# Choosing the passes of a fused attention and FFN kernel two ahead instead of one, with their scales made at the choice

## Chip, cores and metric

The kernel runs on one core of a Trainium2 chip. The metric is the device time of one execution in microseconds (us), as the median of several runs.

## What is computed

```python
# attention: 8 batches, 8 heads, 512 local + 32 global queries, head size 64
s_g  = scale * q_g @ concat(k_g, k_l).T          # global queries see all keys
s_l  = concat(scale * q_l @ k_g.T,               # local queries see the global keys
              where(|i - j| <= 32, scale * q_l @ k_l.T, -1e9))   # and a band of 65
out  = concat(sm(s_g) @ v_all, sm(s_l) @ v_gl)
# FFN on the 4352 rows x of 512 that come out of it
h = x @ w_in                                     # 512 -> 2048
g = where(h > 0, h, exp(min(h, 0)) - 1)          # ELU
return g @ w_out                                 # 2048 -> 512
```

## The kernel before

Attention and FFN run interleaved on the same engines. TensorE works in 16-bit floats for the FFN: every operand is split into a high and a low f16 part, and three products (high by high, high by low, low by high) are summed. That needs power-of-two scales: one for each block of x, one for each pair of f-tiles of the weights.

**The FFN's stream.** The rows of x make 17 blocks of 256: 16 of local rows and one (number 16) of all global rows. The 2048 columns of the middle layer are 8 steps of 256. A *pass* is one block through the steps of one *group*: "a" is step 0, "b" step 1, "c" steps 2 and 3, "d" steps 4 to 7, "f" all 8. While the weights are still being converted, the first blocks go through passes a, b, c, d, and each waits until the weights of its group are there (`group in tab`). Once the table of "f" exists, every block that has not begun takes one pass f. In a step `ffn1` fills a PSUM tile `h` with 24 matmuls (L300), ScalarE turns it into `g` and `hs` (L310, L311, both scaled by a column of the pass's scale tile `xs`), takes the exponential (L312), VectorE joins the two (L319), ScalarE makes the f16 high part `gh` (L326; in pass f L340 and L341) and VectorE the low part `gl` (L322). `ffn2`, two steps later, multiplies by the second weights (L376; L418 in pass f), and at the end of a pass the sum is scaled and stored (L384, L387).

**The scale tile.** `scales(group, mx)` makes the tile `xs` of a pass with four small GpSimd instructions of 128 partitions by 1 to 8 columns: L521 is what L310 waits for, L522 what L311 waits for, L524 what L326 (and L322) need, L525 what the end of the pass needs. They read the scale of the block (`xm`) and of the weights (`isc` of L217, `wm` and `t` of the group's table). Before, `xs` has four buffers, so a pass's tile has to wait until the pass four earlier has read its own for the last time.

**What sets the order.** `choose()` walks the blocks in order and gives the first one whose split is done and whose next group has a table; it calls `scales` at once. Before, it is called when the last step of the running pass has been issued, so one pass is known ahead. A scheduler then places each instruction in its engine's queue; `scales` is under a raised priority (AHEAD_OF), and each engine runs its queue strictly in that order. GpSimd's queue also holds L703 (it normalises the probabilities `p`, four of 128x224 a time, and TensorE transposes them in L714), L646 and L647 (the same for the global queries), L661 (a memset) and L162 (a clamp of 128x1024 in the conversion of the weights, which VectorE goes on with in L166, L169, L173 and ScalarE in L191).

Of the kernel before, what the change touches and what calls it, by code (L numbers as in the profile page):

```python
# [10 lines left out]
F32 = mybir.dt.float32  # L11
# [11 lines left out]
P = 128  # L23
# [6 lines left out]
NP = NFT // 2  # L30
# [26 lines left out]
def attn_ffn(ctx: ExitStack, tc: tile.TileContext, qT, qgT, kT, vT, w_in, w_out, mask, out):  # L57
# [5 lines left out]
    ffn = ctx.enter_context(tc.tile_pool(name="ffn", bufs=2))  # L63
# [220 lines left out]
    def ffn_stream():  # L284
# [228 lines left out]
            return xh, xl, mx, done  # L513

        def scales(group, mx):
            sc = ffn.tile([P, 3 * NP + 1], F32, name="xs", bufs=4)
            wm, t = tab[group]
            o = GROUPS[group]
            r = slice(*o)
            with tc.high_priority(offset=AHEAD_OF):  # L520
                nc.gpsimd.tensor_scalar(sc[:, r], isc[:, r], mx[:, 2:3], 1.0, ALU.mult, ALU.mult)  # L521
                nc.gpsimd.tensor_scalar(sc[:, 2 * NP + 1 + o[0]:2 * NP + 1 + o[1]], isc[:, r], mx[:, 2:3], -1.0,  # L522
                                        ALU.mult, ALU.mult)
                nc.gpsimd.tensor_scalar(sc[:, NP + o[0]:NP + o[1]], t[:, r], mx[:, 3:4], 1.0, ALU.mult, ALU.mult)  # L524
                nc.gpsimd.tensor_scalar(sc[:, 2 * NP:2 * NP + 1], wm, mx[:, 2:3], 2.0 ** -17, ALU.mult, ALU.mult)  # L525
            return sc

        order = [*range(NBL - 1), NBL, NBL - 1]
        xs = {}
        step = dict.fromkeys(order, 0)  # L530

        def load():
            if "f" in tab:
                n = state.setdefault("sums", 0)
                state["turn"] = not state.get("turn")
                if n < NP and state["turn"]:
                    add_up(n, False)
                    state["sums"] += 1
                n = state.setdefault("cross", 0)
                first = min((GROUPS["abcd"[step[b]]][0] for b in order if 0 < step[b] < 4), default=NP)  # L540
                if n < state["sums"] and not uses[n] and n < first:
                    add_up(n, True)
                    state["cross"] += 1
            for blk in order:
                if blk in ready and blk not in xs and not step[blk] and len(xs) < NX:
                    xs[blk] = split_x(blk)

        def choose():

            for blk in order:  # L550
                if blk in xs and xs[blk][3] and step[blk] < 4:
                    group = "f" if "f" in tab and not step[blk] else "abcd"[step[blk]]
                    if group in tab:
                        step[blk] += 4 if group == "f" else 1
                        xh, xl, mx, _ = xs[blk]
                        seven = [] if group == "f" else None
                        if seven is None:
                            for p in range(*GROUPS[group]):
                                uses[p] += 1
                        return group, blk, xh, xl, scales(group, mx), seven  # L560

        job = None
        left = 0
        while lead[0]:
            load()
            yield True
        while left <= NBL:
            load()
            job = job or choose()
            if job is None:  # L570
                yield True
                continue
            cur, job = job, None
            group, blk = cur[:2]
            lo, hi = GROUPS[group]
            for p in range(lo, hi):
                load()
                yield from ffn1(cur, p)
                if len(pend) > LAG2:
                    yield from ffn2()  # L580
                if p == hi - 1:
                    job = choose()
            if group in "df":
                del xs[blk]
                left += 1
# [226 lines left out]


    f = ffn_stream()
    units = (u for g in "abcd" for u in load_weights(g))
    done = credit = 0
# [93 lines left out]
```

## Time and profile before

| | |
|---|---|
| time, median of 3 runs | 995.57 us (993.61 to 997.8) |
| the profiled execution | 993.12 us, span 991.4 us |
| mean granted clock of TensorE | 0.991 |
| busy share of the span: TensorE / VectorE / ScalarE / GpSimd | 96% / 79% / 68% / 25% |

The time is that of a whole execution; the span goes from its first to its last instruction. The engines are named PE (TensorE matmuls), PEld (its weight loads), DVE (VectorE), ACT (ScalarE), POOL (GpSimd) and SP (the queue that issues most DMAs) in the rows below. "Idle before, <- X" in a row is the time for which the engine did nothing ahead of that instruction, and X is what ended it. A busy share is an average over stages with different limits.

### The profile page before, as it was taken

What the parts mean: (1) busy time and instruction counts of PE and PEld (TensorE: products, weight loads), DVE (VectorE), ACT (ScalarE), POOL (GpSimd) and SP (SyncE); (2) the same over time, 40 slices, a digit from 0 to 9 for tenths busy, and PEclk for the clock granted to TensorE, in tenths of its full rate; (3) what the DMA queues carried; (4) which work ended last, traced back from release to release, by engine and by line L of the source; (5) the groups of instructions that cost most, each with busy time, mean ns of one, the idle gap of its engine ahead of it and who ended that gap; (6) DMA issues with size and microseconds to landing.
All of it is one profiled execution on the core that took longest, in us unless ns stands there. A gap on an engine that the chain in (4) does not pass through costs nothing.

```text
span 991.4 us, 21656 instructions
## 1 busy us (share of the span) xinstructions
PE 954.0 (96%) x8128; PEld 767.2 (77%) x8128; DVE 786.9 (79%) x2233; ACT 678.0 (68%) x1545; POOL 251.8 (25%) x444
## 2 busy tenths in 40 slices
PE   7899879999999999999999999999999999999997
PEld 4576556666667888888888788888888888888886
DVE  5898989999987778787777778787787878776665
ACT  4978777886656666666756666667766766677664
POOL 2656444462311221212211122112211221100000
PEclk9799999999999999999999999999999999999999
DMA  8627665651211023011211023112210100000000
GB/s 282 234 81 264 201 192 185 224 175 44 92 59 59 34 80 107 28 44 70 81 49 28 33 81 108 28 39 75 81 44 13 43 23 33 1 23 22 2 23 22
DMA packets 39360, 81.95 MB, mean 83 GB/s; under 512 B 3896, under 2 KB 6328, under 8 KB 39256
## 3 DMA queue, kind: packets, MB, share of 16 engines
q1 hardware_dynamic: 39064, 80.31, 24.5%
q8 instruction: 64, 1.05, 0.4%
q14 instruction: 40, 0.33, 0.1%
q10 hardware_dynamic: 144, 0.13, 0.0%
q0 software_dynamic: 48, 0.13, 0.0%
HBM read 65.36 MB, written 15.20 MB: 81 GB/s over the span
## 4 chain that ended last, share of the span: by engine, by line
PE 64%; DVE 16%; ACT 10%; issue 6%; DMA 3%; POOL 1%; SPq 0%; POOLq 0%; DVEq 0%; ACTq 0%
PE h L300 24%; PE acc L418 10%; PE h L418 5%; PE pa L736 4%; PE acc L376 4%; PE pa L714 4%; PE pa L677 4%; ACT p L696 3%; PE pa L418 2%; DVE p L689 2%; PE pa L300 2%; PE pa L625 2%; DVE gl L322 2%; DVE g L319 2%; ACT g L310 1%
## 5 line engine op out<-in xcount | busy, mean ns | idle before, releaser
L300 PE MATMUL h<-xh,winh 128*128 128x256 f16 x992 | 271.5, 274 | 10.3 <-ACT hs L311 8.1
L300 PE MATMUL h<-xl,winh 128*128 128x256 f16 x992 | 271.0, 273 | 0.0
L300 PE MATMUL h<-xh,winl 128*128 128x256 f16 x992 | 270.9, 273 | 0.1
L300 PEld LDWEIGHTS <-winh 128*128 128x128 f16 x2176 | 211.4, 99 | 49.4 <-issue 18.1
L703 POOL TENSOR_SCALAR p<-p,sm 128x224 f32<-128x224 f32 x256 | 147.0, 592 | 321.5 <-DVE sm L701 142.2
L319 DVE SCALAR_TENSOR_TENSOR g<-g,hs 128x512 f32<-128x512 f32 x136 | 95.4, 702 | 91.1 <-ACT g L312 90.5
L696 ACT ACTIVATE p<-p,m 128x224 f32<-128x224 f32 x256 | 120.3, 473 | 65.9 <-DVE m L692 65.9
L418 PEld LDWEIGHTS <-gh 128*128 128x128 f16 x1456 | 141.8, 98 | 21.5 <-issue 4.8
L300 PEld LDWEIGHTS <-winl 128*128 128x128 f16 x1088 | 106.7, 98 | 13.5 <-DVE winl L194 0.5
L310 ACT ACTIVATE g<-h,xs 128x512 f32<-128x512 f32 x124 | 84.8, 683 | 45.7 <-PE h L300 40.4
L322 DVE SCALAR_TENSOR_TENSOR gl<-gs,xs,gh 128x640 f16<-128x640 f32 x104 | 94.3, 907 | 22.7 <-ACT gh L341 22.5
L341 ACT ACTIVATE gh<-gs,xs 128x640 f16<-128x640 f32 x104 | 86.3, 830 | 36.5 <-DVE gs L337 36.3
L340 ACT ACTIVATE gh<-g,xs 128x256 f16<-128x256 f32 x104 | 53.2, 512 | 84.4 <-DVE g L319 84.4
L418 PE MATMUL acc<-wouth,gh 128*128 128x256 f16 (+1 forms) x312 | 87.8, 282 | 0.2 <-ACT gh L341 0.2
L312 ACT ACTIVATE g<-g 128x512 f32<-128x512 f32 x136 | 85.7, 632 | 0.0
L311 ACT ACTIVATE hs<-h,xs 128x512 f32<-128x512 f32 x124 | 84.6, 682 | 1.1 <-POOL xs L522 1.1
L418 PE MATMUL acc<-wouth,gl 128*128 128x256 f16 x312 | 85.0, 273 | 0.2 <-DVE gl L322 0.2
L418 PE MATMUL acc<-woutl,gh 128*128 128x256 f16 x312 | 85.0, 273 | 0.0
L714 PE MATMUL pa<-ident,p 128*128 128x128 f32 x512 | 77.9, 277 | 4.4 <-POOL p L703 3.3
L418 PEld LDWEIGHTS <-gl 128*128 128x128 f16 x728 | 71.2, 98 | 12.9 <-DVE gl L322 0.5
L689 DVE CUSTOM_DVE_ANT_0 p<-pa,msk 128x224 f32<-128x224 f32 x228 | 76.9, 384 | 3.0 <-PE pa L677 3.0
L322 DVE SCALAR_TENSOR_TENSOR gl<-g,xs,gh 128x256 f16<-128x256 f32 (+1 forms) x136 | 76.5, 563 | 3.1 <-ACT gh L326 2.9
(206 smaller groups left out, 1952.4 us busy)
## 6 DMA issues: line engine op xcount, KB each, us to landing
v<-vT SPq DMA_DIRECT2D x64, 256.0 KB, 2.7
k<-kT SPq DMA_DIRECT2D x32, 448.0 KB, 4.3
q<-qT SPq DMA_DIRECT2D x32, 256.0 KB, 5.4
raw<-w_in SPq DMA_DIRECT2D x8, 1024.0 KB, 6.2
raw<-w_out SPq DMA_DIRECT2D x8, 1024.0 KB, 5.4
out<-o SPq DMA_DIRECT2D x32, 256.0 KB, 2.1
od<-o SPq DMA_DIRECT2D x24, 256.0 KB, 3.0
o<-od SPq DMA_DIRECT2D x24, 256.0 KB, 3.0
```

Source lines behind the costliest of these rows:

```text
L300: nc.tensor.matmul(h[:, j, :], wt[:, c, f], xt[:, c, :], start=k == 0, stop=k == 11)
L310: nc.scalar.activation(g, hf, AF.Relu, scale=sc[:, p:p + 1])
L311: nc.scalar.activation(hs, hf, AF.Copy, scale=sc[:, 2 * NP + 1 + p:2 * NP + 2 + p])
L312: nc.scalar.activation(g, g, AF.Exp, scale=-1.0)
L319: nc.vector.scalar_tensor_tensor(out=g, in0=g, scalar=-1.0, in1=hs, op0=ALU.add, op1=ALU.max)
L322: nc.vector.scalar_tensor_tensor(out=dst, in0=src, scalar=sg, in1=hi, op0=ALU.mult, op1=ALU.subtract)
L341: nc.scalar.activation(gh[:, 2:7, :], s, AF.Copy, scale=sg)
L418: nc.tensor.matmul(cols, gt, w, start=first, stop=last and k == len(todo) - 1)
L689: nc.vector.tensor_tensor_reduce(out=p[:, 0:KW], in0=sp[r][:, j * KW:(j + 1) * KW], in1=msk[:, mi, :], op0=ALU.add, op1=ALU.max, scale=1.0 ...
L696: nc.scalar.activation(ps[i][:, 0:KW], ps[i][:, 0:KW], AF.Exp, bias=m[:, 1, i:i + 1], scale=scale, accum_out=s[:, 0, i:i + 1])
L703: nc.gpsimd.tensor_scalar(ps[i][:, 0:KW], ps[i][:, 0:KW], s[:, 1, i:i + 1], 1.0, ALU.mult, ALU.mult)
L714: nc.tensor.transpose(tp[:, (2 * r + i) * P:(2 * r + i + 1) * P], ps[2 * j + r][:, i * P:(i + 1) * P], ident)
```

## The change

`scales` gets six buffers instead of four. The single `job` becomes a list `jobs` of up to two, which `look()` fills by calling `choose()` until there are two or none can be chosen. `look()` is called at the top of each round, right after a pass is taken from the list, and after the last step of a pass. So the scales of a pass are issued up to one whole pass earlier.

```diff
         def scales(group, mx):
-            sc = ffn.tile([P, 3 * NP + 1], F32, name="xs", bufs=4)
+            sc = ffn.tile([P, 3 * NP + 1], F32, name="xs", bufs=6)
...
-        job = None
+        jobs = []
         left = 0
+
+        def look():
+            while len(jobs) < 2:
+                job = choose()
+                if job is None:
+                    return
+                jobs.append(job)
+
...
         while left <= NBL:
             load()
-            job = job or choose()
-            if job is None:
+            look()
+            if not jobs:
                 yield True
                 continue
-            cur, job = job, None
+            cur = jobs.pop(0)
+            look()
             group, blk = cur[:2]
...
                 if p == hi - 1:
-                    job = choose()
+                    look()
```

In the order of the built programs TensorE's and VectorE's queues stay the same, instruction for instruction, and so does that of SP's DMAs. GpSimd's queue has the same instructions, moved in the first third of the program only; ScalarE's has one instruction moved. The three places below are all in the stage in which the weights are converted. In the names, `xm_308` is block 0, `xm_583` block 1, `xm_846` block 2; from L562 on the changed file's line numbers are up to 9 higher.

GpSimd, pass b of block 2 (`xs_1554`), before; it stands between two clamps of the weights:

```order
L162 TENSOR_SCALAR cu_1434<-cu_1434 128x1024
L521 TENSOR_SCALAR xs_1554<-isc_133,xm_846 128x1
L522 TENSOR_SCALAR xs_1554<-isc_133,xm_846 128x1
L524 TENSOR_SCALAR xs_1554<-t_b_1234,xm_846 128x1
L525 TENSOR_SCALAR xs_1554<-wm_b_1233,xm_846 128x1
L162 TENSOR_SCALAR cu_1550<-cu_1550 128x1024
```

The same pass's scales now (`xs_1419`), beside those of pass a of block 2 (`xs_1414`):

```order
L521 TENSOR_SCALAR xs_1414<-isc_133,xm_846 128x1
L521 TENSOR_SCALAR xs_1419<-isc_133,xm_846 128x1
L522 TENSOR_SCALAR xs_1414<-isc_133,xm_846 128x1
L522 TENSOR_SCALAR xs_1419<-isc_133,xm_846 128x1
L525 TENSOR_SCALAR xs_1414<-wm_a_392,xm_846 128x1
L524 TENSOR_SCALAR xs_1414<-t_a_393,xm_846 128x1
```

Its L521 and L522 moved some 15 instructions up, ahead of a group of L703; nothing stands between the two clamps any more.

ScalarE at the same pass, before (`h_1559` is block 2's step of pass b):

```order
L387 ACTIVATE o_1463<-acc_1461,xs_1028 128x512
L312 ACTIVATE g_1516<-g_1516 128x512
L310 ACTIVATE g_1593<-h_1559,xs_1554 128x512
L311 ACTIVATE hs_1594<-h_1559,xs_1554 128x512
L161 ACTIVATE cu_1550<-raw_1548 128x1024
L326 ACTIVATE gh_1521<-g_1516,xs_1485 128x512
```

And now:

```order
L387 ACTIVATE o_1473<-acc_1471,xs_973 128x512
L310 ACTIVATE g_1593<-h_1559,xs_1419 128x512
L311 ACTIVATE hs_1594<-h_1559,xs_1419 128x512
L312 ACTIVATE g_1521<-g_1521 128x512
L161 ACTIVATE cu_1555<-raw_1553 128x1024
L326 ACTIVATE gh_1526<-g_1521,xs_1414 128x512
```

The exponential L312 of the step before went behind L310 and L311 of this one.

GpSimd, the first pass c (block 0, `xs_1748`), before:

```order
L162 TENSOR_SCALAR cu_1794<-cu_1794 128x1024
L525 TENSOR_SCALAR xs_1748<-wm_c_1667,xm_308 128x1
L521 TENSOR_SCALAR xs_1748<-isc_133,xm_308 128x2
L522 TENSOR_SCALAR xs_1748<-isc_133,xm_308 128x2
L521 TENSOR_SCALAR xs_1908<-isc_133,xm_583 128x2
L522 TENSOR_SCALAR xs_1908<-isc_133,xm_583 128x2
```

And now, with the scales of passes c of blocks 1 and 2 (`xs_1753`, `xs_1758`) in the same place:

```order
L162 TENSOR_SCALAR cu_1804<-cu_1804 128x1024
L525 TENSOR_SCALAR xs_1748<-wm_c_1667,xm_308 128x1
L521 TENSOR_SCALAR xs_1748<-isc_133,xm_308 128x2
L521 TENSOR_SCALAR xs_1753<-isc_133,xm_583 128x2
L521 TENSOR_SCALAR xs_1758<-isc_133,xm_846 128x2
L522 TENSOR_SCALAR xs_1753<-isc_133,xm_583 128x2
L522 TENSOR_SCALAR xs_1758<-isc_133,xm_846 128x2
L522 TENSOR_SCALAR xs_1748<-isc_133,xm_308 128x2
```

L521 of block 0 keeps its place behind the clamp; its L522 moved from third to seventh in the row.

## Rows read from the trace of the kernel before

**Rows 1.** The page, busy time of the engines.
```profile
PE 954.0 (96%) x8128; PEld 767.2 (77%) x8128; DVE 786.9 (79%) x2233; ACT 678.0 (68%) x1545; POOL 251.8 (25%) x444
```
**Rows 2.** Stretches: us, busy us (instructions) of each engine, TensorE's granted clock, DMA.
```profile
core 0: us, PE busy (x) PEld busy (x) DVE busy (x) ACT busy (x) POOL busy (x), PEclk, DMA share, GB/s
120.00:130.00 10.00, 8.03 (x55) 4.87 (x54) 10.00 (x23) 6.17 (x10) 2.18 (x2) 1.00 0.78 242
...
170.00:200.00 30.00, 26.91 (x189) 17.83 (x187) 29.96 (x62) 25.41 (x49) 12.88 (x10) 1.00 0.62 204
...
250.00:300.00 50.00, 50.00 (x381) 35.08 (x380) 45.76 (x110) 30.04 (x77) 11.17 (x19) 1.00 0.24 79
```
**Rows 3.** ScalarE's waits for scales: us in total, times, longest us.
```profile
ACT g L310 <- POOL xs L521: 5.0, 2, 3.5
...
ACT hs L311 <- POOL xs L522: 1.1, 1, 1.1
```
**Rows 4.** Timeline of ScalarE at block 2's pass b: start us, us, instruction.
```profile
113.18 0.64 ACT L312 ACTIVATE g<-g 128x512 f32<-128x512 f32 x1
115.33 0.69 ACT L310 ACTIVATE g<-h,xs 128x512 f32<-128x512 f32 x1 [1.52 <-POOL xs L521]
...
118.72 0.70 ACT L326 ACTIVATE gh<-g,xs 128x512 f16<-128x512 f32 x1
```
**Rows 5.** Timeline of GpSimd, the same place.
```profile
113.46 1.84 POOL L521 TENSOR_SCALAR xs<-isc,xm 128x1 f32<-128x1 f32 x1 [4.47 <-ACT o L387]
```
**Rows 6.** Timeline of VectorE, the same place.
```profile
115.17 0.68 DVE L319 SCALAR_TENSOR_TENSOR g<-g,hs 128x512 f32<-128x512 f32 x1
...
119.45 1.02 DVE L322 SCALAR_TENSOR_TENSOR gl<-g,xs,gh 128x512 f16<-128x512 f32 x1 [0.68 <-ACT gh L326]
```
**Rows 7.** Timeline of SP, the load that L161 at 117.66 reads.
```profile
107.72 0.38 SPq L152 DMA_DIRECT2D raw<-w_out  x1
```
**Rows 8.** Tile raw, its loads from 90 to 150 us.
```profile
DMA to landing us min/median/max: 4.9/5.4/6.9
```
**Rows 9.** Timeline of GpSimd at the first pass c.
```profile
137.33 1.96 POOL L162 TENSOR_SCALAR cu<-cu 128x1024 f32<-128x1024 f32 x1
139.37 0.27 POOL L525 TENSOR_SCALAR xs<-wm_c,xm 128x1 f32<-128x1 f32 x1
139.60 0.27 POOL L521 TENSOR_SCALAR xs<-isc,xm 128x2 f32<-128x2 f32 x1
139.85 0.27 POOL L522 TENSOR_SCALAR xs<-isc,xm 128x2 f32<-128x2 f32 x1
```
**Rows 10.** Timeline of ScalarE, the same place.
```profile
139.91 0.69 ACT L310 ACTIVATE g<-h,xs 128x512 f32<-128x512 f32 x1 [3.50 <-POOL xs L521]
140.49 0.68 ACT L311 ACTIVATE hs<-h,xs 128x512 f32<-128x512 f32 x1
```
**Rows 11.** Timeline of TensorE, the same place.
```profile
141.22 0.37 PE L300 MATMUL h<-xh,winh 128*128 128x256 f16 x1 [4.66 <-ACT hs L311]
```
**Rows 12.** Timeline of VectorE, the same place.
```profile
135.44 0.37 DVE L217 TENSOR_SCALAR isc<-pww 128x2 f32<-128x2 f32 x1
...
140.41 0.28 DVE L115 TENSOR_REDUCE xm<-pa 128x1 f32<-128x128 f32 x1
142.88 0.69 DVE L319 SCALAR_TENSOR_TENSOR g<-g,hs 128x512 f32<-128x512 f32 x1 [2.20 <-ACT g L312]
```
**Rows 13.** Stretches around TensorE's longest wait, columns as in rows 2.
```profile
137.00:141.00 4.00, 0.00 (x0) 0.00 (x0) 3.68 (x6) 1.09 (x2) 3.83 (x9) 1.00 0.37 81
141.00:145.00 4.00, 3.78 (x20) 2.70 (x20) 0.76 (x2) 3.55 (x7) 2.98 (x10) 0.57 0.66 250
```
**Rows 14.** Timeline of GpSimd, later places with scales.
```profile
172.78 3.01 POOL L521 TENSOR_SCALAR xs<-isc,xm 128x2 f32<-128x2 f32 x1 [5.14 <-DVE cm L189]
...
209.54 2.71 POOL L703 TENSOR_SCALAR p<-p,sm 128x224 f32<-128x224 f32 x4 [1.59 <-DVE sm L701]
```
**Rows 15.** Timeline of TensorE, the wait after the scales that move up.
```profile
111.59 0.28 PE L300 MATMUL h<-xh,winh 128*128 128x256 f16 x1 [2.05 <-ACT winh L191]
```

## The prediction

> **What bounds the kernel now.** I read the page first. TensorE is busy for 96% of the span and GpSimd, the engine that makes the scales, for 25% [rows 1], so an edit on GpSimd can only count where someone waits for it. The table of stretches then shows two regimes. While the weights are converted, VectorE is full: 10.00 of 10 us from 120 to 130 and 29.96 of 30 from 170 to 200, with TensorE at 8.0 and 26.9 [rows 2]. From 250 us on TensorE is full, 50.00 of 50 [rows 2]. In the first regime an edit is worth what it gives VectorE (or what it adds to a wait that stops all engines); in the second, what it gives TensorE.
>
> Next the waits of ScalarE, because L310, L311 and L326 are what reads the scales as they come. It stood still for GpSimd's scales three times in the whole execution: twice for L521, 5.0 us together, and once for L522, 1.1 us [rows 3]. All three lie in the first regime, at two places: 1.52 us at 115.33 and the 1.1 us behind it, block 2's pass b [rows 4], and 3.50 us at 139.91, the first pass c [rows 10]. Their sum, about 6.1 us or 0.6% of the span, is the most that earlier scales could give directly.
>
> **The change, part by part.** Before and after have the same instructions, and TensorE, VectorE and SP run them in the same order. So nothing is removed or added but waits; what counts is where the scales stand in GpSimd's queue, and the one swap on ScalarE.
>
> *Block 2's pass b (115 us).* L521 started at 113.46 because it waited 4.47 us for L387: its tile was the buffer that the pass four earlier still had to read [rows 5]. With six buffers, and at its new place beside the scales of pass a, it is done by about 100 us. L310 then starts where L312 stood, at 113.18 [rows 4], L311 follows 0.58 later (the spacing of 139.91 and 140.49 [rows 10]), L312 0.57 behind that at 114.33, ending at 114.97. Two things can spoil it. VectorE's L319 at 115.17 needs that L312 [rows 6]: a margin of 0.20 us. And L161, which came after at 117.66, needs its load: issued at 107.72 [rows 7], landed 4.9 to 6.9 us later [rows 8], by 114.6 at the latest, and it would be wanted at about 114.9. So L161 and then L326 move up by some 2.7 us, from 118.72 to about 116.0 (L326 needs L319, over at 115.85). That much is ScalarE's gain, but ScalarE isn't the limit here. VectorE idled 0.68 us for that L326 before L322 at 119.45 [rows 6], and this is all that it gets back, since it has had work to do up to 118.77. From there to the next place it is full, so the 0.68 us carry on. Value **-0.68**; bounds: 0, if the load or L312 comes late, and -2.57 (1.52 and 1.05), if ScalarE's wait were on the path in full.
>
> *The first pass c (140 us).* Here TensorE stops for 4.66 us, its longest wait in this stage: its next 24 matmuls want the PSUM tile that L311 empties [rows 11]. L311 ran at 140.49, right behind L310, which had waited 3.50 us for L521 at 139.60 [rows 9, 10]. Choosing the pass earlier can't help: its weights' scale `isc` is only there at 135.8 [rows 12], and by then GpSimd has four L703 and the clamp L162 (137.33 to 139.3) in front of the scales, in the same order before and after. What does change is behind L521. The scales of three passes c are now chosen together, and block 0's L522, which L311 needs, went from the third to the seventh place counted from L525 at 139.37. One such instruction starts 0.23 to 0.25 us after the other [rows 9], so the seventh starts at 139.37 + 6 x 0.235 = 140.78 and ends at 141.05 (0.27 long). L311 starts then, not at 140.49: 0.56 us late. ScalarE, TensorE (which waits for L311) and VectorE (idle 2.20 us for the L312 behind it [rows 12]) all move by it. Value **+0.56**. Bounds: 0, if the scheduler's queue hides it, and for the other end the slowest L521 of the trace, 3.01 us instead of 0.27 [rows 14], four times: 11 us. I take the low value because the two scales at this place took 0.27 each beside the same work on VectorE [rows 9], and because VectorE runs out of work at 140.7, waiting for ScalarE [rows 12].
>
> The row of 3.01 us is explained by a rule of the Trainium skill (SBUF — State Buffer, "Who interferes with whom"): VectorE and GpSimd share a pair of SBUF ports, an instruction of VectorE with two inputs in SBUF shuts out a GpSimd instruction that reads SBUF, and whichever comes later is blocked for the whole of the other. It speaks against any change that piles scales up beside VectorE's two-input conversions. By the rule the four extra scales cost 0.24 each here, since VectorE's last work ahead of its wait is reductions of one input, and the sum stays at +0.56; by the slowest row it would be +11.6.
>
> *TensorE's clock.* Around this wait the granted clock was 1.00 from 137 to 141, with TensorE idle, and 0.57 from 141 to 145 [rows 13], between the two levels of 1.2 and 2.4 GHz. That cost 4 x 0.43 = 1.7 us. The wait starts 0.68 earlier and ends 0.12 earlier, so it is longer by 0.56, and I leave this price as it is: value 0, bounds -1.7 (gone) and +1.7 (twice as long).
>
> *The other moves.* Two scales (0.47 us) now stand ahead of four L703 at 96 us, so the transposes that read these come up to 0.3 us later; TensorE has a wait of 2.05 us for ScalarE's weights after that, at 111.59, which swallows it [rows 15]. Without that cover it would cost 0.3 us. In the passes d the scales of three blocks are issued at 207.44: four more instructions, 0.95 us, ahead of L703 at 209.54, ahead of which GpSimd idled 1.59 us [rows 14]. The scales of block 3's passes no longer stand between clamps from 153 to 180; nobody waited for them, and VectorE is full there, so this gives nothing. From the passes f on, GpSimd's order is the same, and so nothing changes in the last two thirds.
>
> *Sum:* -0.68 + 0.56 = -0.12 us. The profiled execution took 993.12 us with a span of 991.4, so its like would be 993.0. The median of the runs is 2.45 above that execution; with the same -0.12 it becomes 995.4. A measurement of this kernel can tell about 0.5%, 5 us, from no change (its own three runs lie 4.2 apart).
>
> **The rivals.**
> 1. *No gain, only the loss.* The load or L312 comes late at 115 us, VectorE idles as before, and the +0.56 stays: 996.1. It is a matter of 0.2 us of margin, so it is quite possible; it ends within 0.5% as well.
> 2. *All scale waits vanish (faster).* If the table's own time were not what holds L521 at 139.60, the three waits of 6.07 us would go, with the slow stretch of the clock that follows the longest: 995.57 - 6.07 - 1.7 = 987.8. For it: the rows name the scales as what ended these waits [rows 3]. Against it: L521 of pass c has the same clamp ahead of it in the order, and `isc` comes at 135.8 [rows 12]. It would decide only if L521 ran before the clamp, at about 136.
> 3. *The pile of scales at pass c is slow (slower).* If each of the four extra instructions took 3.01 us as at 172.78 [rows 14], L311 would start at 141.05 + 4 x 2.77 = 152.1, 11.6 late; less the 0.68, and with 1.7 for a longer slow clock, 995.57 + 12.6 = 1008. It decides (over 5 us) from about 1.5 us for each. For it: L521 and L522 took 1.2 to 3 us at several places of this stage. Against it: not here [rows 9], and VectorE empties at that moment.
>
> **How the numbers follow.** The forecast as summed: 0.55. Rival 1: 0.23, together 0.78 within 0.5%. Rival 2 and whatever else could shorten this stage by 5 us: 0.11. Rival 3 and whatever else could lengthen it so (two queues that fall out of step, a clock that stays low): 0.11. The predicted time is that of the likeliest, 995.4. The range adds to it the bounds of the small terms and the spread of the runs: low 995.57 - 2.57 - 2 = 991, high 995.57 + 0.56 + 1.7 + 2 = 1000. Rivals 2 and 3 in full lie outside it, with no more than 2 in 10.
>
> **What would show it.** In the changed kernel's profile ScalarE waits for scales once, not three times: nothing at 113 to 118, and L310 still some 3.5 us at the first pass c. VectorE's idle time of 0.68 us before L322 is gone. TensorE's longest wait there, for L311, grows from 4.66 to about 5.2 us, with ScalarE's L311 itself waiting about 0.5 us for L522, and its end comes at about 141.1. The clock falls once behind it as before. From 205 us on both traces run alike with an offset of under 1 us. The prediction is wrong if L521 of pass c starts before 138 us, if the scales there take over 1 us each, or if a wait shows up on GpSimd's queue ahead of L162 or L703 that delays a conversion or a transpose by more than its idle time.

## The result and the profile after

The changed kernel took 998.01 us (median of 20 runs, 995.52 to 1001.26) beside 995.27 us for the kernel before (993.61 to 997.8): ratio 1.0027, 95% interval 1.0017 to 1.0036. It is slower by about 2.7 us. That lies inside the forecast range and under the 0.5% that I had taken as the limit of a measurement, but the twenty runs tell 0.1% apart, and no loss was forecast. The same kernel, measured twice more, came out at 1.0005 (0.9993 to 1.0018) and 1.0024 (1.0013 to 1.0035). Weighted by their intervals the three give about 1.002: some 2 us. They differ by more than their intervals suggest, though, so a ratio of 1.001 to 1.002 that rests on one measurement is weak by itself. (The ratios are taken over the runs; they need not be the quotient of the two medians.)

The profiled execution after had a span of 999.5 us at a mean granted clock of 0.985. It is the slowest of the twenty runs (1001.26 us), so not every wait in it is the change's. Its page, busy time of the engines, for [rows 1]:

```profile
PE 957.8 (96%) x8128; PEld 769.8 (77%) x8128; DVE 786.7 (79%) x2233; ACT 678.4 (68%) x1545; POOL 246.9 (25%) x444
```

VectorE and ScalarE do the same work as before to within 0.4 us, so what was lost there is waiting; TensorE was busy 3.8 us longer, at the lower clock. ScalarE's waits for scales (us in total, times, longest), for [rows 3]:

```profile
ACT g L310 <- POOL xs L521: 2.9, 1, 2.9
ACT gh L326 <- POOL xs L524: 1.0, 1, 1.0
ACT hs L311 <- POOL xs L522: 0.5, 1, 0.5
```

They fell from 6.1 to 4.4 us, and the kernel got slower: one of the three is new (L524), and the larger losses stand on another engine. Block 2's pass b went as forecast; ScalarE and VectorE there, for [rows 4, 6]:

```profile
116.88 0.78 ACT L310 ACTIVATE g<-h,xs 128x512 f32<-128x512 f32 x1
117.45 0.79 ACT L311 ACTIVATE hs<-h,xs 128x512 f32<-128x512 f32 x1
```
```profile
122.48 0.74 DVE L322 SCALAR_TENSOR_TENSOR gl<-g,xs,gh 128x512 f16<-128x512 f32 x1
```

Neither L310 nor L322 waits. At the first pass c the order worked as forecast too (its clock comes further down); GpSimd, ScalarE, TensorE, for [rows 9 to 11]:

```profile
141.47 1.96 POOL L162 TENSOR_SCALAR cu<-cu 128x1024 f32<-128x1024 f32 x1
143.51 0.27 POOL L525 TENSOR_SCALAR xs<-wm_c,xm 128x1 f32<-128x1 f32 x1
143.75 0.75 POOL L521 TENSOR_SCALAR xs<-isc,xm 128x2 f32<-128x2 f32 x3
144.47 0.75 POOL L522 TENSOR_SCALAR xs<-isc,xm 128x2 f32<-128x2 f32 x3
```
```profile
144.05 0.69 ACT L310 ACTIVATE g<-h,xs 128x512 f32<-128x512 f32 x1 [2.89 <-POOL xs L521]
145.25 0.69 ACT L311 ACTIVATE hs<-h,xs 128x512 f32<-128x512 f32 x1 [0.51 <-POOL xs L522]
```
```profile
145.99 0.37 PE L300 MATMUL h<-xh,winh 128*128 128x256 f16 x1 [5.03 <-ACT hs L311]
```

L311 now starts 1.20 us after L310 instead of 0.58 [rows 10], so it is 0.62 us late, and TensorE's wait grew from 4.66 [rows 11] to 5.03 us.

What the forecast did not hold comes right behind it. GpSimd and VectorE from 150 us, where the scales of block 3's passes a and b now stand:

```profile
150.97 0.57 POOL L521 TENSOR_SCALAR xs<-isc,xm 128x1 f32<-128x1 f32 x1 [2.86 <-DVE xm L109]
151.51 1.33 POOL L522 TENSOR_SCALAR xs<-isc,xm 128x1 f32<-128x1 f32 x1
152.81 4.22 POOL L525 TENSOR_SCALAR xs<-wm_a,xm 128x1 f32<-128x1 f32 x1
157.00 0.26 POOL L521 TENSOR_SCALAR xs<-isc,xm 128x1 f32<-128x1 f32 x1
...
157.47 0.26 POOL L525 TENSOR_SCALAR xs<-wm_b,xm 128x1 f32<-128x1 f32 x1
...
158.28 1.04 POOL L162 TENSOR_SCALAR cu<-cu 128x1024 f32<-128x1024 f32 x1
```
```profile
152.77 0.74 DVE L322 SCALAR_TENSOR_TENSOR gl<-g,xs,gh 128x512 f16<-128x512 f32 x1
153.43 1.22 DVE L169 SCALAR_TENSOR_TENSOR cu<-raw,cu 128x1024 int32<-128x1024 int32 x1
154.56 1.28 DVE L507 SCALAR_TENSOR_TENSOR xl<-xr,xm,xh 128x1024 f16<-128x1024 f32 x1
155.76 1.22 DVE L173 SCALAR_TENSOR_TENSOR cu<-raw,cu 128x1024 int32<-128x1024 int32 x1
...
159.36 0.69 DVE L166 TENSOR_SCALAR cu<-cu 128x1024 int32<-128x1024 int32 x1 [0.88 <-POOL cu L162]
```

An L525 on one column, 0.26 us where nothing disturbs it, took 4.22 us: it began 0.04 us after VectorE's L322 and ended when the fourth of VectorE's two-input instructions in a row was over (L173, 156.98); the scale behind it started at 157.00. The clamp L162 stands behind it and five more scales in the queue, and VectorE, full until then, waits 0.88 us for the clamp at L166. What the clamp reads had been there for 2.4 us; ScalarE's L161:

```profile
154.74 1.15 ACT L161 ACTIVATE cu<-raw 128x1024 f32<-128x1024 f32 x1
```

In the kernel before, the same clamp stood ahead of block 3's scales and began as soon as its L161 was done, and VectorE's L166 did not wait:

```profile
150.52 2.16 POOL L162 TENSOR_SCALAR cu<-cu 128x1024 f32<-128x1024 f32 x1 [6.03 <-ACT cu L161]
```
```profile
153.20 0.69 DVE L166 TENSOR_SCALAR cu<-cu 128x1024 int32<-128x1024 int32 x1
```

Back in the kernel after, some of VectorE's L322 (the last two at the passes d), then GpSimd's clamps:

```profile
172.72 1.45 DVE L322 SCALAR_TENSOR_TENSOR gl<-g,xs,gh 128x512 f16<-128x512 f32 x1
178.59 0.72 DVE L322 SCALAR_TENSOR_TENSOR gl<-g,xs,gh 128x512 f16<-128x512 f32 x1
183.97 1.52 DVE L322 SCALAR_TENSOR_TENSOR gl<-g,xs,gh 128x512 f16<-128x512 f32 x1
...
228.44 2.36 DVE L322 SCALAR_TENSOR_TENSOR gl<-g,xs,gh 128x512 f16<-128x512 f32 x2 [0.85 <-ACT gh L326]
```
```profile
171.82 1.80 POOL L162 TENSOR_SCALAR cu<-cu 128x1024 f32<-128x1024 f32 x1 [4.28 <-ACT cu L161]
183.59 1.36 POOL L162 TENSOR_SCALAR cu<-cu 128x1024 f32<-128x1024 f32 x1 [9.96 <-ACT cu L161]
```

An undisturbed L322 of this form takes 0.72 us; the two that begin while a clamp runs take 1.45 and 1.52, twice as long. Before had one such meeting in this stretch, of 1.23 us at 166.95. The clamps have shifted because block 3's scales no longer stand between them. And 0.85 us of VectorE's idle time at 228 us is new: it waits for L326, which waits for L524 (the 1.0 us above). Before, these two L326 waited for nothing:

```profile
219.73 1.35 ACT L326 ACTIVATE gh<-g,xs 128x512 f16<-128x512 f32 x2
```

One more wait is at its longest in this profile: ScalarE's L161 at 128.52 waited 1.84 us for a load of the weights, and VectorE's L194 at 131.20 1.58 us behind it. Eight other profiles of kernels with the earlier pass b of block 2 have it too, with 0.2 to 1.0 us; no profile without that move has it.

### The profile page after: what moved, and what is told of

Read it like the earlier page. It is cut to its first block, busy times and chain, and to the rows that moved or that the text cites. A ratio compares the mean times of both kernels' runs of the same rounds, so it can differ in the third digit from the quotient of the medians.

```text
span 999.5 us, 21649 instructions
## 1 busy us (share of the span) xinstructions
PE 957.8 (96%) x8128; PEld 769.8 (77%) x8128; DVE 786.7 (79%) x2233; ACT 678.4 (68%) x1545; POOL 246.9 (25%) x444
## 4 chain that ended last, share of the span: by engine, by line
PE 64%; DVE 16%; ACT 9%; issue 6%; DMA 4%; POOL 1%; POOLq 0%; DVEq 0%; ACTq 0%; SPq 0%
PE h L300 23%; PE acc L418 10%; PE h L418 5%; PE pa L745 4%; PE acc L376 4%; PE pa L723 4%; PE pa L686 3%; ACT p L705 3%; PE pa L418 2%; DVE p L698 2%; PE pa L300 2%; PE pa L634 2%; DVE gl L322 2%; DVE g L319 2%; DMA raw<-w_out 1%
## 5 line engine op out<-in xcount | busy, mean ns | idle before, releaser
L319 DVE SCALAR_TENSOR_TENSOR g<-g,hs 128x512 f32<-128x512 f32 x136 | 95.9, 705 | 91.4 <-ACT g L312 90.7
L310 ACT ACTIVATE g<-h,xs 128x512 f32<-128x512 f32 x124 | 85.1, 686 | 44.2 <-PE h L300 41.2
L322 DVE SCALAR_TENSOR_TENSOR gl<-gs,xs,gh 128x640 f16<-128x640 f32 x104 | 94.2, 906 | 22.8 <-ACT gh L341 22.5
L341 ACT ACTIVATE gh<-gs,xs 128x640 f16<-128x640 f32 x104 | 86.3, 830 | 36.3 <-DVE gs L337 36.2
L312 ACT ACTIVATE g<-g 128x512 f32<-128x512 f32 x136 | 85.8, 633 | 0.0
L311 ACT ACTIVATE hs<-h,xs 128x512 f32<-128x512 f32 x124 | 84.9, 684 | 0.5 <-POOL xs L522 0.5
L322 DVE SCALAR_TENSOR_TENSOR gl<-g,xs,gh 128x256 f16<-128x256 f32 (+1 forms) x136 | 76.3, 561 | 2.9 <-ACT gh L326 2.9
```

Of the source, the lines that this page charges most:

```text
L310: nc.scalar.activation(g, hf, AF.Relu, scale=sc[:, p:p + 1])
L311: nc.scalar.activation(hs, hf, AF.Copy, scale=sc[:, 2 * NP + 1 + p:2 * NP + 2 + p])
L312: nc.scalar.activation(g, g, AF.Exp, scale=-1.0)
L319: nc.vector.scalar_tensor_tensor(out=g, in0=g, scalar=-1.0, in1=hs, op0=ALU.add, op1=ALU.max)
L322: nc.vector.scalar_tensor_tensor(out=dst, in0=src, scalar=sg, in1=hi, op0=ALU.mult, op1=ALU.subtract)
L341: nc.scalar.activation(gh[:, 2:7, :], s, AF.Copy, scale=sg)
```

## The experiments

Four theories:

- **A.** With six buffers, scales of block 3 overtake other work in GpSimd's queue: the clamp L162 at 154 to 159 us, and L524 of the first passes d. VectorE waits for what they overtook.
- **B.** ScalarE runs block 2's pass b earlier and so into its next weight load.
- **C.** The look-ahead itself loses: at the first pass c L522 of block 0 is seventh.
- **D.** Tiles lie elsewhere in SBUF, since six buffers take 200 bytes more.

In the order of the built programs, six buffers alone make all the moves of A and B; two passes of look-ahead alone only some at the first passes c and d. Each time stands beside runs of the kernel before on the same chip.

**Six buffers alone.**
```diff
-            sc = ffn.tile([P, 3 * NP + 1], F32, name="xs", bufs=4)
+            sc = ffn.tile([P, 3 * NP + 1], F32, name="xs", bufs=6)
```


> Six buffers alone; passes are still chosen one ahead. Theory A (the loss is made in GpSimd's queue, at three places: the clamp L162 behind block 3's scales at about 153 us, L522 of the first pass c, L524 of the passes d): the six buffers already move block 2's pass b (about -0.7 us) and put block 3's scales ahead of L162 and one more pair ahead of L524 (about +0.9 and +0.5), so 0 to +1.5 us against before, with VectorE waiting some 0.9 us for L162 in the trace. Theory B (the earlier ScalarE at 115 us runs into its weight load, which costs 1.5 us and more, and the queue is innocent): +1.5 us or more here, and VectorE waits 1.5 us for ScalarE's L191 at about 127 us. Theory C (the look-ahead is the whole loss): no slower than before, -0.7 us.

997.98 us against 994.85, ratio 1.0031 (1.0019 to 1.0042): the whole loss, with no look-ahead. It is twice what theory A had allowed, and the time would suit B; but the wait that B asked for, 1.5 us of VectorE for ScalarE's L191, is not in the trace, and A's 0.88 us at L166 is.

**The look-ahead alone** (the change with `bufs=4`).

> Passes chosen two ahead, but with four buffers. Block 2's pass b and block 3's scales then stand where they stood before; L522 of the first pass c is two places later, and the scales of three passes d stand together. Theory A: +0.1 us at pass c and +0.5 to +1.2 at the passes d, so +0.5 to +1.3 us. Theory B: as before, within 0.3 us. Theory C: the whole loss, +2.5 us or more.

995.45 us, ratio 1.0003 (0.9993 to 1.0014): no measurable loss, and C falls for what the look-ahead does alone. With four buffers only two passes are in the row at the first pass c, though, and L311 is just 0.14 us late (0.72 us behind L310); a run below has the full row.

**Six buffers, with two passes ahead only while the passes c run, and only from the passes d on.**
```diff
-            while len(jobs) < 2:
+            while len(jobs) < (2 if "c" in tab and "d" not in tab else 1):
```
(For the second, `"d" in tab`; the `look()` behind `jobs.pop(0)` stands under the same condition.)

> Six buffers, and two ahead only while the table of c is there and that of d is not; against e1 only block 0's L522 of pass c moves, four places back. Theory A: +0.6 us over e1, up to +1.3 if TensorE's clock stays low for longer; L311 of pass c waits 0.5 us for L522. Theory B: as e1. Theory C: most of the loss is here or in e4.

> Six buffers, and two ahead only once the table of d is there; against e1 only the scales of the passes d move: those of blocks 1 and 2 ahead of a group of four normalisations, and L524 of block 2 ahead of that of block 1. Theory A: +0.5 to +1.2 us over e1, with ScalarE's L326 waiting about 1 us for L524. Theory B: as e1.

997.95 us, 1.0031 (1.0018 to 1.0044), and 997.67 us, 1.0032 (1.0016 to 1.0049): no more than six buffers alone, where theory A had expected +0.6 us and +0.5 to +1.2 us more. The 0.61 us at L311 is there in the first (1.20 us behind L310), but too small to show in the time.

**Two spare tiles: the SBUF of six buffers, the queue of four.**
```diff
+    for _ in range(2):
+        spare = ffn.tile([P, 3 * NP + 1], F32, name="spare", bufs=2)
+        nc.gpsimd.memset(spare, 0.0)
```


> The kernel before with the SBUF of six buffers, but with four of them used: two spare 128x25 tiles of the scales' size are written once at the start, and the order of every queue is that of before. Theory A (the loss of e1_six_buffers, +0.31% or 3.1 us, comes from scales that move ahead in GpSimd's queue): no change, ratio within 0.999 to 1.001. Theory D (it comes from where the tiles of the scales lie in SBUF, since all tiles allocated behind them move by 200 bytes): about +3 us, ratio 1.002 to 1.004.

994.31 us against 994.44, ratio 1.0006 (0.9996 to 1.0017). Theory D falls.

**Own tiles for single passes.** Each takes the kernel before and lets the scales of one place alone go ahead.
```diff
-            sc = ffn.tile([P, 3 * NP + 1], F32, name="xs", bufs=4)
+            own = (group, blk) == ("b", 2)
+            sc = ffn.tile([P, 3 * NP + 1], F32, name="xo" if own else "xs", bufs=2 if own else 4)
```
(For the others `own` is true of passes a and b of block 3, of pass d of block 3, and of all three, these with `bufs=3`. In the first three of these kernels the scales' lines are one higher: L522 to L526 for L521 to L525.)

> The kernel before with a tile of its own for the scales of block 2's pass b alone: these scales go ahead in GpSimd's queue, ScalarE's L310 runs without its wait, and a third block's scales join the pile at the first pass c. Block 3's scales stay behind the clamp L162. Theory A (the loss stands at block 3's clamp and at the passes d): no loss here, by the two terms of the forecast -0.68 + 0.56 us, ratio 0.9985 to 1.0005, and no VectorE wait for the clamp at L166 of 0.88 us. Theory B (the earlier pass b of block 2 runs into the load and so is the loss): +2 to +3 us, ratio 1.002 to 1.003. Theory D: no move of the layout but 200 bytes, so +3 us as well if it counts.

> The kernel before with tiles of their own for the scales of block 3's passes a and b alone: only these move ahead of the clamp L162 in GpSimd's queue. Theory A: VectorE waits 0.88 us for that clamp at L166 as in e1_six_buffers, and the loss is +0.9 us there or more where the full VectorE stage passes it on; ratio 1.0008 to 1.0025. Theories B and D: B gives no change (0.999 to 1.0005), D +3 us (1.002 to 1.004) with or without that wait.

> The kernel before with a tile of its own for the scales of block 3's pass d alone: its L525 and L524 stand ahead of L524 of block 0's pass d. Theory A: ScalarE's L326 waits about 1 us for L524 there and VectorE's L322 behind it 0.85 to 1.08 us as in e1_six_buffers; +1 us, ratio 1.0005 to 1.002. Theory B: no change, 0.999 to 1.0005. Theory D: +3 us, 1.002 to 1.004.

> The kernel before with tiles of their own for the scales of block 3's passes a, b and d, and for no others. Theory A: the two losses add, 0.14% and 0.13% by the two kernels that have one each, so ratio 1.0017 to 1.0037, with VectorE's wait of 0.88 us at L166, its wait of about 1 us at L322 of the passes d, and one or two L322 between 165 and 185 us at 1.45 to 1.52 us in place of 0.73, since a clamp of GpSimd now meets them. Theory G (what is lost needs block 2's earlier pass b as well): no more than 1.001.

| own tile for | us, against before | ratio (95%) |
|---|---|---|
| block 2, pass b | 993.60, 994.44 | 0.9994 (0.9984 to 1.0004) |
| block 3, passes a and b | 996.09, 994.44 | 1.0014 (1.0004 to 1.0024) |
| block 3, pass d | 995.23, 994.44 | 1.0013 (1.0003 to 1.0023) |
| block 3, passes a, b and d | 997.39, 994.89 | 1.0019 (1.0009 to 1.0028) |

Block 2's earlier pass b does no measurable harm: B falls as the cause, though ScalarE does run into its weight load here (1.02 us, and 0.84 of VectorE behind it). Each place of A alone has a ratio whose interval just leaves out 1, in one measurement each; all three together lose as much as the change. With passes a and b of block 3 alone, GpSimd and VectorE:

```profile
149.67 4.21 POOL L526 TENSOR_SCALAR xo<-wm_a,xm 128x1 f32<-128x1 f32 x1
...
155.14 1.04 POOL L162 TENSOR_SCALAR cu<-cu 128x1024 f32<-128x1024 f32 x1
```
```profile
156.22 0.69 DVE L166 TENSOR_SCALAR cu<-cu 128x1024 int32<-128x1024 int32 x1 [0.88 <-POOL cu L162]
```

The same row of VectorE in the kernel with the spare tiles, whose order is that of before:

```profile
153.95 0.68 DVE L166 TENSOR_SCALAR cu<-cu 128x1024 int32<-128x1024 int32 x1
```

It waits for nothing there. With pass d of block 3 alone, GpSimd, ScalarE and VectorE at the passes d (`xo` is block 3's tile):

```profile
217.34 0.27 POOL L522 TENSOR_SCALAR xo<-isc,xm 128x4 f32<-128x4 f32 x1
217.58 0.84 POOL L523 TENSOR_SCALAR xo<-isc,xm 128x4 f32<-128x4 f32 x1
...
220.27 1.23 POOL L526 TENSOR_SCALAR xs<-wm_d,xm 128x1 f32<-128x1 f32 x3
221.48 1.23 POOL L526 TENSOR_SCALAR xo<-wm_d,xm 128x1 f32<-128x1 f32 x1
222.68 0.74 POOL L525 TENSOR_SCALAR xs<-t_d,xm 128x4 f32<-128x4 f32 x3
```
```profile
222.98 1.33 ACT L326 ACTIVATE gh<-g,xs 128x512 f16<-128x512 f32 x2 [1.24 <-POOL xs L525]
```
```profile
223.74 1.75 DVE L322 SCALAR_TENSOR_TENSOR gl<-g,xs,gh 128x512 f16<-128x512 f32 x2 [1.08 <-ACT gh L326]
```

Three added instructions of block 3, of 0.27, 0.84 and 1.23 us, stand ahead of what L326 needs, and L326 waits 1.24. With all three tiles, VectorE waited 0.40 us at L166 and 1.08 at that L322, and one L322 took 1.53 us at a clamp.

**The look-ahead with an own tile for block 2's pass b** (the change with `bufs=4` and the edit above).

> The changed kernel with four buffers in place of six and a tile of its own for the scales of block 2's pass b: the whole look-ahead, block 2's scales early, but block 3's scales behind the clamp L162 and those of its pass d behind L703 as in before. Theory A (the loss of the change stands only where six buffers let block 3's scales overtake): no loss, ratio 0.9985 to 1.0005, VectorE without the waits of 0.88 us at L166 and of 0.85 to 1.08 us at L322. Theory G (look-ahead and earlier scales lose together, though neither does alone): ratio of the changed kernel, 1.0017 to 1.0036.

994.88 against 994.89 us, ratio 1.0003 (0.999 to 1.0017), with L522 seventh: C falls here too, to within 0.17%. Without block 3's overtaking nothing measurable is lost, and nothing measurable is won; theory G, named in these expectations, falls.

**A scale of the weights made earlier, for the passes c.** The second rival said that the long wait at the first pass c would go if L521 ran before the clamp, and that this was out of reach because `isc` comes late. This moves `isc`.
```diff
-        t = wts.tile([P, NP], F32, name=f"t_{group}")
+        t = wts.tile([P, NP], F32, name=f"t_{group}"); nc.vector.tensor_scalar_mul(isc[:, r], pww[:, r], -2.0 ** -28) if group == "c" else None
...
-            nc.vector.tensor_scalar_mul(isc[:, r], pww[:, r], -2.0 ** -28)
+            if group != "c": nc.vector.tensor_scalar_mul(isc[:, r], pww[:, r], -2.0 ** -28)
```


> The kernel before with one line moved: the scale isc of the weights of group c is made with their maximum instead of five steps later, so that L521 and L522 of the first two passes c can stand ahead of the clamp L162 in GpSimd's queue; the scheduler then also orders some instructions of ScalarE and VectorE of this stage anew. Theory E (the second rival of the forecast: the 3.50 us wait of L310 at the first pass c is on the path, and the fallen clock behind it): L310 without a wait there, TensorE's 4.66 us for L311 down to under 2 us, clock of 141 to 145 at 0.8 or more, -2.5 to -5.2 us, ratio 0.9948 to 0.9975. Theory F (VectorE, full on both sides of that place, takes the gain up): 0.999 to 1.001.

> The same moved line, and a tile of its own for block 2's pass b: no wait of ScalarE for scales anywhere. Theory E: 0.6 us better than with the moved line alone, ratio 0.994 to 0.997, which would beat both kernels. Theory F: 0.9985 to 1.0005.

> The changed kernel with the scale isc of group c made with the weights' maximum, as in e11_isc_early_for_c, which came out at 0.9958. If the loss of six buffers comes with any order of the stage (block 3's scales overtake clamps and L703 here too): 0.9958 plus 0.0027, ratio 0.997 to 0.9995. If it hangs on where the clamps stand in the order of before: 0.9945 to 0.997, no worse than e11.

In the kernel before 991.11 against 994.89 us, ratio 0.9958 (0.9942 to 0.9974); with block 2's tile 0.9968 (0.9954 to 0.9982); in the changed kernel 992.07 against 995.00, 0.9964 (0.995 to 0.9978). The first beats both kernels; block 2's tile did not add the 0.6 us expected of it. The three don't differ beyond their intervals, so in this order of the stage no loss of the change shows. GpSimd and ScalarE at the first pass c, in the kernel before with `isc` early, and its stretches:

```profile
131.81 0.27 POOL L521 TENSOR_SCALAR xs<-isc,xm 128x2 f32<-128x2 f32 x1 [4.13 <-DVE m L692]
...
143.09 1.36 POOL L162 TENSOR_SCALAR cu<-cu 128x1024 f32<-128x1024 f32 x1
```
```profile
134.20 0.67 ACT L310 ACTIVATE g<-h,xs 128x512 f32<-128x512 f32 x1
```
```profile
137.00:141.00 4.00, 3.58 (x31) 2.87 (x30) 4.00 (x8) 4.00 (x10) 4.00 (x7) 1.00 0.12 23
141.00:145.00 4.00, 4.00 (x32) 3.04 (x32) 2.93 (x9) 3.79 (x6) 3.83 (x5) 1.00 0.99 323
```

L521 runs at 131.81, L310 waits for nothing, TensorE's long wait for L311 is gone (it was busy for 0.00 of the 4 us from 137 to 141 before), and its clock stays at 1.00 from 141 to 145, where it was 0.57 [rows 13].

**The change twice more, and six buffers again.**

> The changed kernel once more. If the late load at 128 us belongs to the change, ScalarE's L161 there waits 1 to 2 us for raw again and VectorE's L194 at about 131 us 1.58 us behind it. If it belongs to the one execution, neither shows, L310 and L311 of the first pass c stand 1.4 us earlier against the pass before, and the two L322 between 165 and 190 us at 1.45 to 1.52 us, the wait of 0.88 us at L166 and that of 0.85 to 1.08 us at L322 of the passes d remain. Time ratio 1.0017 to 1.0036 in both cases.

> The changed kernel beside six buffers alone, on one chip. If the waits come and go by execution: both kernels at the same ratio within their intervals, 1.001 to 1.0035; the wait of 0.88 us at L166 in both profiles, the wait of 0.85 to 1.08 us at L322 of the passes d in one, both or neither. If the look-ahead takes back part of the loss: the changed kernel at 1.000 to 1.0015 and six buffers alone 0.002 above it.

> Six buffers alone once more, for the same comparison: 1.0019 to 1.0042 by its first measurement; if the waits come and go by execution the two kernels agree, else this one stands 0.002 above the changed kernel.

The change: 995.43 against 995.00 us and 996.44 against 994.30; six buffers 997.62, ratio 1.0036 (1.0022 to 1.005). The first, 1.0005, lies below what was expected. In both new profiles of the change the load at 128 us costs ScalarE under 0.3 us and VectorE nothing, and the wait at the passes d is not there; both have the others (at L166 the second has 0.64 us in place of 0.88). In the first of them VectorE, and ScalarE at the passes d:

```profile
154.12 0.69 DVE L166 TENSOR_SCALAR cu<-cu 128x1024 int32<-128x1024 int32 x1 [0.88 <-POOL cu L162]
167.38 1.44 DVE L322 SCALAR_TENSOR_TENSOR gl<-g,xs,gh 128x512 f16<-128x512 f32 x1
178.62 1.53 DVE L322 SCALAR_TENSOR_TENSOR gl<-g,xs,gh 128x512 f16<-128x512 f32 x1
```
```profile
221.18 1.35 ACT L326 ACTIVATE gh<-g,xs 128x512 f16<-128x512 f32 x2
```

So these two waits come and go from execution to execution in the changed kernel; the others stand in all three of its profiles. Whether the look-ahead takes back part of what six buffers lose stays open: 1.0024 against 1.0036 on one chip, with intervals that overlap.

**All profiles side by side.** The first third of a profile shifts by up to 4 us with its start-up: the first L310 of the stage starts at 71.98 us in the profile before and between 72.92 and 76.00 in the others, ahead of all that the change moves. So I took the distances between L310s at six places (in the profile before at 108.21, 139.91, 147.10, 170.55, 192.93 and, for the passes d, 216.57 to 238.46). Each number is the difference of two starts, in us; from 192.93 to 216.57 all have 23.64 to 23.67, and from 238.46 to the end all take 753 us to within 0.6, so the differences are made in between. The last column is the mean granted clock of TensorE over the 8 us from the L310 of the first pass c (139.91 before).

| kernel | 108 to 140 | 140 to 147 | 147 to 171 | 171 to 193 | passes d | 108 to 238 | clock |
|---|---|---|---|---|---|---|---|
| before | 31.70 | 7.19 | 23.45 | 22.38 | 21.89 | 130.25 | 0.79 |
| spare tiles | 31.76 | 7.08 | 22.42 | 22.40 | 21.89 | 129.20 | 0.79 |
| look-ahead alone | 31.74 | 7.03 | 23.23 | 22.40 | 21.73 | 129.78 | 0.79 |
| look-ahead, own tile, block 2 b | 31.40 | 7.46 | 23.20 | 22.41 | 21.63 | 129.75 | 0.79 |
| own tile, block 2 b | 31.37 | 6.90 | 23.25 | 22.39 | 21.90 | 129.48 | 0.79 |
| own tiles, block 3 a, b | 31.73 | 7.57 | 24.31 | 23.13 | 21.91 | 132.31 | 0.66 |
| own tile, block 3 d | 31.73 | 7.57 | 23.25 | 22.39 | 22.79 | 131.39 | 0.66 |
| own tiles, block 3 a, b, d | 31.76 | 8.45 | 23.92 | 23.17 | 22.81 | 133.76 | 0.57 |
| six buffers | 30.73 | 7.69 | 24.10 | 22.38 | 22.83 | 131.38 | 0.64 |
| six buffers again | 30.69 | 7.70 | 24.25 | 23.15 | 22.81 | 132.24 | 0.64 |
| six buffers, ahead in c | 31.30 | 7.65 | 24.14 | 23.15 | 22.83 | 132.73 | 0.79 |
| six buffers, ahead in d | 30.67 | 8.02 | 24.14 | 23.18 | 22.80 | 132.46 | 0.60 |
| the change | 32.14 | 8.50 | 24.01 | 23.14 | 23.03 | 134.48 | 0.58 |
| the change again | 30.66 | 8.46 | 23.91 | 23.18 | 21.85 | 131.70 | 0.58 |
| the change, third | 30.66 | 8.74 | 23.80 | 23.17 | 21.56 | 131.57 | 0.57 |

The columns show the gain of 0.3 to 1.0 us at block 2's pass b (32.14 is the profile with the late load), then a loss of 0.4 to 1.1 us where block 3's scales overtake the clamp, 0.75 where an L322 meets a clamp, and 0.9 where block 3's pass d overtakes L524, each only in kernels that have that move, the last two not in every profile of them. A column can also vary with no move at all: the spare tiles have the order of before and 22.42 for 23.45. The first five kernels move none of block 3's scales; their sums are 129.2 to 130.3, mean 129.7. The change without its two passing waits lies at 131.6 and 131.7, some 1.9 us above. (The highest sums, 134.48 and 133.76, come from executions that were the slowest of their kernel's runs.)

The largest single loss in the change's three profiles, 1.3 to 1.6 us, stands from 140 to 147, though, and only 0.61 us of it is a scale that moved. The rest goes with the clock, which was low for longer in nine of the ten profiles of kernels that move block 3's scales, and in none of the others. The order can't be the whole reason: the three kernels with own tiles for block 3 have the order of before up to that place. Nor does the clock explain the measured times. Over the timed runs its mean was 0.989 with own tiles for passes a and b and 0.988 with one for pass d, beside 0.988 for the kernel before; 0.988 with all three, beside 0.987. So these kernels are slower at a clock that is no lower. (With six buffers it was the same as before in the first measurement and 0.001 lower in the second.) Why the profiles divide as they do stays open.

## Why the forecast was wrong, point by point

*Block 2's pass b: right.* Forecast -0.68 us; L322's idle time of 0.68 [rows 6] is gone. The distance 108 to 140 shrank by 1.0 us in five profiles with six buffers and by 0.3 to 0.4 in three others with this move; the forecast lies between. In time the move alone gave -0.8 us of the medians, ratio 0.9994, which can't be told from 1. ScalarE's larger gain was not on the path, as argued.

*The first pass c: right in mechanism and size for the order.* Forecast +0.56; L311 is 0.61 to 0.62 late wherever L522 stands seventh. No kernel with this move and none of block 3's has a measurable loss (1.0003 with its own tile for block 2 and the look-ahead, where L311 starts 1.19 us after L310).

*The clock: not borne out as 0, though within its bounds.* In the profile after, the granted clock was 0.50 from 145 to 150 us; over the 8 us from L310 it was 0.57 to 0.58 in all three profiles of the change and 0.79 before. The distance 140 to 147 is 7.5 and 7.7 us with L522 seventh and the clock at 0.79, and 8.5 to 8.7 in the change: 0.8 to 1.3 us for the clock, under the bound of 1.7. How much of it belongs to the change is open.

*"The scales of block 3's passes no longer stand between clamps ... nobody waited for them, and VectorE is full there, so this gives nothing": the step that failed.* It asked who waits for the moved instructions, and not what they would now stand ahead of. They stand ahead of a clamp. The term stood in the sum at 0; VectorE waited 0.64 to 0.88 us for that clamp in the three profiles of the change, and the distance 147 to 171 grew there by 0.4 to 0.8 us against the 23.20 to 23.45 of five kernels without this move. VectorE being full made it worse: it is the reader of that clamp, and its two-input conversions are what stretches the scales. The third rival had that price, 3.01 us for one [rows 14], at the wrong place: at the first pass c the added scales took 0.25 us each, as forecast; at block 3 one took 4.22. The Trainium skill (SBUF — State Buffer, "Who interferes with whom") says that a VectorE instruction with two SBUF inputs and a GpSimd instruction that reads SBUF exclude each other, the later one being held for the whole of the other. The rows agree, in both directions: L525 beside VectorE's L322, L169, L507 and L173, and L322 beside L162, 1.45 for 0.72 us. They go further than that sentence in one point: L525 was held through four instructions in a row. I had weighed this rule only where I expected the pile.

*The two scales at 96 us: nothing, as forecast.* From the first L310 to that at 108 the profiles of the change have 35.2 to 36.3 us, kernels without this move 35.0 to 36.2.

*"Four more instructions, 0.95 us, ahead of L703 ... ahead of which GpSimd idled 1.59 us": incomplete, and so the passes d were missed.* The pile at 207.44 was covered: it took 1.9 us and not 0.95 in the change, and still the distance from 192.93 to 216.57 is the same everywhere. But more scales came behind later L703, next to what L326 waits for, and these were not in the sum. One of them beside VectorE's two-input run took 1.23 us, not 0.24, and had no cover.

*The rivals.* The first can't be told from the forecast by time, but the traces speak against it: VectorE's idle time before L322 is gone in every profile with the earlier pass b. The second was right about the place: with L521 ahead of the clamp the wait and the slow clock went. Its price was 7.8 us for all three waits and the clock; the one move gave 3.8 by the medians, at the place of the longest wait, and VectorE then waits 0.87 us for the delayed clamp. My objection, that `isc` comes late, held for this change, which doesn't move `isc`. The third was right that GpSimd's scales can be slow and cost time, and wrong in place and size.

*What would show it.* "From 205 us on ... an offset of under 1 us" was wrong (1.3 to 4.2 us more from 108 to 238 than before), and the warning named in the forecast came true: a wait on GpSimd's queue ahead of L162 that delays a conversion.

By the ratios, theory A's two places are worth 0.14% and 0.13% alone and 0.19% together. That is the size of the change's loss and over half of what six buffers lose (0.31% and 0.36%); whether the rest of the latter is noise or another cause the intervals do not show.

## What to carry to other kernels

An instruction that nobody waits for still has a price when it moves up in an in-order queue: look at what it now stands ahead of, who reads that, and how long it can be held there, by the slowest of its kind beside the work that will then run next to it. Deeper buffering moves the work of every user of the tile, also at places where nothing waited; a tile of its own for the one late user took away the same wait without that (a gain in time, 0.9994, could not be told from none). And before a consumer's queue is rearranged, ask for the input that comes last: here one early small instruction gave 3.8 us where the whole look-ahead gave nothing measurable.

## What the runs showed that I had not expected

- A GpSimd instruction on one column was held 4.22 us through four VectorE instructions in a row, in the change and, with 4.21 us, in the kernel that moves only block 3's passes a and b. It is not always so long: the L521 at 113.46 of the kernel before [rows 5] was through after two such instructions, 1.84 us.
- It works the other way too: VectorE's L322 of 0.72 us took 1.44 to 1.53 us, in nine profiles, when it began during a clamp of GpSimd.
- Whether such a meeting happens hangs on less than a tenth of a microsecond. At the passes d of the change, block 0's L524 began, by the records, 0.10, 0.12 and 0.10 us ahead of VectorE's L319 in its three profiles; in the first it was held for 2.03 us, and the wait stood behind it, in the others it took 0.27.
